# Moving PE drains, moving Gram matmuls, and loading fewer columns in a ConvNeXt V2 block

## The chip, the cores and the metric

The kernel runs on one core of a Trainium2 chip. The metric is the time of one execution on the device in microseconds (us), as the median of several runs. Engines are named as in the profile: PE does matmuls, ACT activations, DVE and POOL elementwise work, SP issues transfers. POOL issues some transfers too, and each issue takes POOL's own time.

Two kinds of numbers appear. Times of kernels are medians of several runs. Places inside a kernel (when a phase starts, how long a block takes) come from the trace of one profiled run, whose span is some 2 us shorter than the time of the same run.

## The reference, cut to what matters

```python
def reference(x, dw, w1, w2, grn_gamma, grn_beta):     # x: 1 x 512 x 512 x 96, bf16
    out = zeros_like(x)
    for i in range(3):
        for j in range(3):
            out = out + xp[:, i:i+H, j:j+W, :] * dw[i, j]   # depthwise 3x3
    h = _layernorm(out, axis=-1)
    h = gelu(einsum('bhwc,ce->bhwe', h, w1))               # 96 -> 384, tanh form
    gx = sqrt((h * h).sum(axis=(1, 2), keepdims=True) + 1e-6)   # over the whole image
    nx = gx / (gx.mean(axis=-1, keepdims=True) + 1e-6)
    h = grn_gamma * (h * nx) + grn_beta + h
    return x + einsum('bhwe,ec->bhwc', h, w2)              # 384 -> 96
```

The sum over the whole image splits the kernel into two phases. Nothing of the last product can be finished before every pixel has been expanded and squared once.

## The kernel before

The image is cut into 128 blocks of four rows. The first phase goes through slots. A full slot convolves one block on PE (`Y`, evacuated by ACT as `y_bf`), and expands an earlier block with `w1` on PE (`U`) and GELU on ACT. The six GELUs of a slot are three `gsh` (channels on partitions, their squares summed by DVE) and three `gm` (pixels on partitions; their squares are summed by Gram matmuls on PE into `SG`). Normalised rows `yn`, and one quarter of the GELU results (`g_dram`), go to DRAM. The last 14 slots have no convolution left.

This is the order of PE's work in a slot (`mlp` part, cut):

```python
conv(0)
if not taps:                      # a slot without convolution
    for b2 in get("gram"):
        if b2 != b:
            gram_mms(b2)          # 12 or 24 matmuls over the gm of the block before
pair(0)                           # U -> gsh0
pair(1)                           # U -> gsh1
squares(0)
conv(1)
...
pair(2)                           # U -> gsh2
...
conv(2)
if evac: evac()                   # y_bf
rest(0)                           # U -> gm0
...
rest(1)
if taps: ... gram_mms(b2) ...     # a slot with convolution has its Gram here
rest(2)
```

`U` has two buffers. Each burst of convolution matmuls uses small tiles (64 rows x 32 columns of PE), the rest uses all 128x128. The burst:

```python
def burst(n):
    k = sum(len(ms) for ms in mms[:n])
    if n:
        pe.drain()
    for h, j, i, dx in mms[n]:
        ...
        pe.matmul(Y[i][32 * j:32 * j + 32, o0:o1], lhsT=Wq[...], rhs=..., ...)
```

The second phase goes through 128 blocks. For each, SP and POOL load what was kept (`gl`), the normalised rows (`ynT`) and the input (`xr`); POOL adds the bias (`xb`); PE expands the three quarters that were not kept (`U`), ACT applies GELU (`gr`), PE multiplies with `W2s` (`O`), DVE adds `xb` (`o_sb`), SP stores. The loads and POOL's addition:

```python
def yn_rows(q):
    return yn_dram[q:q + 2].rearrange("q c w -> (q c) w")[0:128]

def stage_load(n, sq, pq):                      # sq is SP, pq is POOL
    ...
    kept = late.gl.tile([128, 1, NCH, QW], bf16, name="gl")
    (pq if q % 3 == 0 else sq).dma_start(
        out=kept[:].rearrange("p t j w -> p (t j w)"), in_=g_dram[q])
    ynt = yn_ring[v]
    sq.dma_start(out=ynt[:].rearrange("p r w -> p (r w)"), in_=yn_rows(q))
    ...
    xr = late.xr.tile([128, PXP, C], bf16, name="xr")      # 5 buffers
    pq.dma_start(out=xr[:], in_=x[0, r0:r0 + GR]...)
```

A pacing rule decides how far the expansions run ahead of the multiplications. A unit is one third of a block's expansion (one `gr`); there are 384 (`total`), four calls a block, and `LEAD` is 8:

```python
def pace(n, sub):
    due = sum(1 for v in todo if v <= n + 1) if sub == NSUB - 1 else 0
    even = LEAD + (n * NSUB + sub + 1) * total / (NSUB * NBLK)
    advance(max(due, even), n + PRE)
```

## Time and profile before

The time before is 1587.96 us (three runs, 1584.48 to 1589.34).

| Part | From | To | What repeats |
|---|---|---|---|
| Slots with convolution | start | 943 us | 7.54 us a slot |
| 14 slots without | 943 us | 1041 us | mostly 6.80 us a slot |
| Second phase | 1049 us | 1581 us | 4.2 us a block |

The first two lines of the page of before, span and busy time of each engine:

```profile
span 1581.4 us, 55730 instructions
PE 1461.4 (92%) x23749; PEld 845.8 (53%) x23749; DVE 1129.2 (71%) x2027; ACT 1461.4 (92%) x1306; POOL 1316.3 (83%) x933
```

These are averages over parts with different limits. The windows view of before shows two of the parts, one from the slots with convolution and one from the second phase:

```profile
core 0: us, PE busy (x) PEld busy (x) DVE busy (x) ACT busy (x) POOL busy (x), PEclk, DMA share, GB/s
400.00:600.00 200.00, 189.08 (x3402) 95.41 (x3401) 171.96 (x293) 190.46 (x187) 176.73 (x138) 1.00 0.78 240
1100.00:1300.00 200.00, 198.21 (x2780) 143.38 (x2777) 105.92 (x194) 198.32 (x147) 185.10 (x112) 1.00 1.03 411
```

In the second phase, PE and ACT are 99% busy, the DMA engines' share is 1.03 (packets overlap, so it can exceed 1), and POOL is 93% busy.

The timeline view shows order and starts. Its columns are start, duration, engine, line, operation, output and inputs, count, and in brackets the idle time before with its cause. A line may hold several instructions. First PE in a full slot of before:

```profile
600.34 0.87 PE L32 MATMUL Y<-xT,Wq 64*32 64x512 bf16 x24
601.15 1.09 PE L32 MATMUL U<-ynT,w1p 128*128 128x512 bf16 x4
602.35 0.87 PE L32 MATMUL Y<-xT,Wq 64*32 64x512 bf16 x24
```

The first burst ends at 600.34 + 0.87 = 601.21 and the expansion behind it starts at 601.15, 0.06 us earlier. That is a switch of tile size without a drain. The expansion ends at 602.24 and the second burst, which has a drain in front, starts at 602.35, 0.11 us later. Ends of matmuls are not observed: the Trainium skill, "Perfetto Trace Analysis", section "Tensor Engine Instruction (MATMUL, LD_WEIGHTS)", says that the profiler estimates them. So only the difference of the two gaps is used, some 0.17 us. Starts are observed, and over all slots with convolution they say (medians, worked out from the trace): behind a 512-column matmul of an expansion the next matmul starts after 0.22 us where the tile size stays.

ACT in the same slot of before:

```profile
598.75 2.85 ACT L32 ACTIVATE gm<-U 128x1024 bf16<-128x1024 f32 x3
601.84 2.97 ACT L32 ACTIVATE gsh<-U 128x1024 bf16<-128x1024 f32 x3 [0.24 <-ACT gm L32]
604.88 1.45 ACT L32 ACTIVATE y_bf<-Y 128x1536 bf16<-128x1536 f32 x1
```

ACT waits 0.24 us before the first `gsh`, and three `gsh` take 2.97 us where three `gm` take 2.85, so there is a hidden wait among them. One GELU alone has a duration of 1.02 us, but three take 2.85: records of neighbours overlap, and the share of busy time hides short waits.

In the slots without convolution, ACT of before:

```profile
959.03 2.85 ACT L32 ACTIVATE gsh<-U 128x1024 bf16<-128x1024 f32 x3 [3.78 <-issue]
961.76 2.88 ACT L32 ACTIVATE gm<-U 128x1024 bf16<-128x1024 f32 x3
965.83 2.86 ACT L32 ACTIVATE gsh<-U 128x1024 bf16<-128x1024 f32 x3 [1.19 <-issue]
```

ACT waits 1.19 us in front of every `gsh0`. PE's order is the cause. Its timeline in before shows the Gram matmuls (`SG`), which need the last `gm`, in front of the expansion that `gsh0` needs:

```profile
963.77 0.40 PE L32 MATMUL SG<-gm 128*128 128x128 bf16 x4 [0.32 <-ACT gm L32]
964.69 0.62 PE L32 MATMUL SG<-gm 128*128 128x128 bf16 x8 [0.52 <-ACT gm L32]
965.15 1.03 PE L32 MATMUL U<-ynT,w1p 128*128 128x512 bf16 x4
```

In the second phase, POOL of before:

```profile
1179.71 3.14 POOL L277 TENSOR_TENSOR xb<-xr,B2c 128x1536 f32<-128x1536 bf16 x1
1183.14 0.55 POOL L249 DMA_DIRECT2D xr<-in_x_dram  x1 [0.30 <-POOL xb L277]
1183.69 0.54 POOL L244 DMA_DIRECT2D gl<-g_dram  x1
1184.25 3.14 POOL L277 TENSOR_TENSOR xb<-xr,B2c 128x1536 f32<-128x1536 bf16 x1
```

Each issue of `xr` re-uses a buffer that the addition just in front of it has read, so it waits for that addition's semaphore: 0.30 us, on POOL's own work. The Trainium skill, "GPSIMD Engine Reference", section "Instruction dispatch", says that the next POOL instruction may begin before all of the engine's cores are done with the one before, so a dependency needs a wait for the semaphore. The trace agrees: without such a wait, the next instruction starts between 0.07 us before and 0.02 us after the end of the one before; with it, 0.30 us after. The issue itself occupies POOL for 0.55 us.

### The profile page before, as it was taken

To read this page: it belongs to the slowest core of one execution; us is meant where nothing else is said; L and a number is where in the kernel's file an instruction comes from. 1 tells how busy PE (TensorE), PEld (TensorE's weight loads), DVE (VectorE), ACT (ScalarE), POOL (GpSimd) and SP (SyncE) were. 2 spreads that over 40 slices of the span, in tenths; PEclk is the share of its full clock that TensorE was granted. 3 is DMA by queue.
4 is the path that set the end of the run, shared out by engine and by line. 5 is a ranking of instruction groups with operands and counts; after the bars stand their busy time and mean duration, and the time that the engine had idled before them with its cause. 6 is when DMAs were issued, how large, how long until landed. Compare 5 with 4: busy or idle time off the path is not lost. (4 is left out here: it accounts for less than half of the span.)

```text
span 1581.4 us, 55730 instructions
## 1 busy us (share of the span) xinstructions
PE 1461.4 (92%) x23749; PEld 845.8 (53%) x23749; DVE 1129.2 (71%) x2027; ACT 1461.4 (92%) x1306; POOL 1316.3 (83%) x933
## 2 busy tenths in 40 slices
PE   7889999999999999999999986689999999999998
PEld 2434444444444444444444443357777676676766
DVE  6848978888888888888898877755555555555545
ACT  3879999999999999999999997899999999999997
POOL 3559888989989898988989896349999999899997
PEclk8999999999999999999999999999999999999999
DMA  5668787787777787787778666679999999999996
GB/s 146 180 186 264 226 260 212 237 258 227 232 235 246 218 261 222 227 246 239 216 235 254 196 193 200 202 253 412 412 412 412 409 410 408 405 409 408 409 408 259
DMA packets 186654, 444.45 MB, mean 281 GB/s; under 512 B 34054, under 2 KB 83302, under 8 KB 186406
## 3 DMA queue, kind: packets, MB, share of 16 engines
q1 hardware_dynamic: 171156, 373.10, 70.1%
q0 software_dynamic: 13888, 67.64, 10.9%
q8 instruction: 186, 3.05, 0.8%
q14 instruction: 62, 0.51, 0.1%
q10 hardware_dynamic: 1362, 0.15, 0.1%
HBM read 289.30 MB, written 150.72 MB: 278 GB/s over the span
## 5 line engine op out<-in xcount | busy, mean ns | idle before, releaser
L32 PE MATMUL U<-ynT,w1p 128*128 128x512 bf16 x2166 | 606.1, 381 | 17.5 <-ACT gsh L32 13.2
L32 DVE BATCH_NORM_STATS2 bst<-gsh 128x6 f32<-128x512 bf16 x756 | 468.5, 673 | 145.5 <-ACT gsh L32 145.5
L32 ACT ACTIVATE gr<-U 128x1536 bf16<-128x1536 f32 (+1 forms) x384 | 521.1, 1453 | 11.1 <-PE U L32 8.1
L32 POOL TENSOR_TENSOR yn<-y_bf,rbc 128x1536 bf16<-128x1536 bf16 x128 | 397.0, 3104 | 87.0 <-DMA rbc<-r_dram 39.8
L32 DVE TENSOR_TENSOR o_sb<-O,xb 128x384 bf16<-128x384 f32 x512 | 277.4, 556 | 251.2 <-PE O L32 181.2
L277 POOL TENSOR_TENSOR xb<-xr,B2c 128x1536 f32<-128x1536 bf16 x126 | 394.7, 3134 | 47.8 <-DVE B2c L32 44.8
L32 ACT ACTIVATE gsh<-U 128x1024 bf16<-128x1024 f32 x378 | 370.3, 1022 | 50.5 <-ACT gm L32 17.3
L32 ACT ACTIVATE gm<-U 128x1024 bf16<-128x1024 f32 x384 | 367.9, 1032 | 0.1
L32 PE MATMUL Y<-xT,Wq 64*32 64x511 bf16 (+1 forms) x8694 | 323.4, 389 | 35.0 <-DVE B2bc_f L32 3.7
L32 POOL TENSOR_TENSOR ysq<-y_bf 128x1536 bf16<-128x1536 bf16 x114 | 313.1, 2747 | 17.8 <-ACT y_bf L32 17.4
L32 PEld LDWEIGHTS <-w1p 128*128 128x128 bf16 x2166 | 168.1, 98 | 243.7 <-issue 161.0
L32 PEld LDWEIGHTS <-gr 128*128 128x128 bf16 x4584 | 236.3, 98 | 109.1 <-issue 26.4
L32 PE MATMUL O<-W2s,gr 128*128 128x96 bf16 x4584 | 256.8, 206 | 11.0 <-DVE o_sb L32 9.2
L32 PEld LDWEIGHTS <-Wq 64*32 64x32 bf16 x9216 | 105.9, 91 | 227.2 <-issue 188.9
L32 ACT ACTIVATE y_bf<-Y 128x1536 bf16<-128x1536 f32 x121 | 175.5, 1450 | 24.9 <-PE Y L32 17.8
L32 PE MATMUL U<-w1p,ynT 128*128 128x384 bf16 (+2 forms) x1032 | 161.4, 272 | 34.0 <-ACT gm L32 29.9
L32 DVE STREAM_TRANSPOSE xT<-xin 128x576 f32<-128x576 f32 (+1 forms) x256 | 181.4, 747 | 4.0 <-DMA xin<-in_x_dram 3.0
L32 DVE BATCH_NORM_STATS2 bst<-gm 128x6 f32<-128x512 bf16 x252 | 156.5, 676 | 1.5 <-ACT gm L32 1.5
L32 PE MATMUL SG<-gm 128*128 128x128 bf16 x2064 | 139.6, 220 | 11.1 <-ACT gm L32 8.5
L32 PEld LDWEIGHTS <-ynT 128*128 128x128 bf16 x1032 | 88.8, 97 | 90.4 <-issue 69.2
L32 PEld LDWEIGHTS <-gm 128*128 128x128 bf16 x2064 | 120.9, 98 | 23.8 <-ACT gm L32 13.7
L249 POOL DMA_DIRECT2D xr<-in_x_dram x123 | 68.1, 553 | 35.9 <-POOL xb L277 35.6
(103 smaller groups left out, 694.0 us busy)
## 6 DMA issues: line engine op xcount, KB each, us to landing
ynT<-yn_dram SPq DMA_DIRECT2D x126, 512.0 KB
xin<-in_x_dram SPq DMA_DIRECT2D x126, 432.0 KB
yn_dram<-yn SPq DMA_DIRECT2D x512, 96.0 KB
ynT<-yn_dram SPq DMA_DIRECT2D x128, 384.0 KB
xr<-in_x_dram POOLq DMA_DIRECT2D x128, 384.0 KB, 6.7
out_dram<-o_sb SPq DMA_DIRECT2D x128, 384.0 KB
g_dram<-gsh SPq DMA_DIRECT2D x126, 384.0 KB
gl<-g_dram SPq DMA_DIRECT2D x84, 384.0 KB
```

Source lines behind the costliest of these rows:

```text
L32: r = f(*a, **k)
L249: pq.dma_start(out=xr[:], in_=x[0, r0:r0 + GR].rearrange("r w c -> (r w) c").rearrange("(p g) c -> p g c", g=PXP))
L277: pq.tensor_tensor(out=xb[:], in0=grp[q]["xr"][:], in1=bias[:, None, :].to_broadcast([128, PXP, C]), op=ALU.add)
```

## The change

The intent: take the cost of draining PE out of the place where a convolution burst waits to begin; let ACT start the next slot's `gsh0` before Gram is done; load only those columns of `yn` that the second phase expands; spread the expansions so that they last until nearly the end; and store the last block in quarters. Five hunks (cut at each `...`; the new helper `out_part` and the last `stage_out`, which goes, are left out):

```diff
 # columns
     def yn_rows(q):
-        return yn_dram[q:q + 2].rearrange("q c w -> (q c) w")[0:128]
+        k = kept_quads(q) * 128
+        return yn_dram[q:q + 2].rearrange("q c (r w) -> (q c) r w", r=GR)[0:128, :, k:]
 ...
-                sq.dma_start(out=ynt[:].rearrange("p r w -> p (r w)"), in_=yn_rows(q))
+                sq.dma_start(out=ynt[:, :, kept_quads(q) * 128:], in_=yn_rows(q))
 # pacing
-            even = LEAD + (n * NSUB + sub + 1) * total / (NSUB * NBLK)
+            even = LEAD + (n * NSUB + sub + 1) * (total + 2 - LEAD) / (NSUB * NBLK)
 # drains
             def burst(n):
                 k = sum(len(ms) for ms in mms[:n])
-                if n:
-                    pe.drain()
                 for h, j, i, dx in mms[n]:
 ...
                     k += 1
+                if n < 2:
+                    pe.drain()
 # Gram
                 conv(0)
+                pair(0)
+                pair(1)
                 if not taps:
                     for b2 in get("gram"):
                         if b2 != b:
                             gram_mms(b2)
-                pair(0)
-                pair(1)
 # output
+                if n == NBLK - 1:
+                    out_part(q, o_sb, sub)      # stores a quarter of the last block
 ...
+            if n == NBLK - 1:
+                stage_out(*held)                # the block before goes out first
+                held = None
```

More of the change, by code (lines that the diff above doesn't have):

```diff
@@ L885, with out_part @@
         dve2.tensor_copy(out=B2c[:], in_=B2bc_f[:])
+        def out_part(q, o_sb, sub):
+            r0 = q * GR
+            nc.sync.dma_start(
+                out=out[0, r0:r0 + GR].rearrange("r w c -> (r w) c").rearrange(
+                    "(p g) c -> p g c", g=PXP)[:, sub * GPS:(sub + 1) * GPS],
+                in_=o_sb[:, sub * GPS:(sub + 1) * GPS])
         held = None
@@ L896 @@
             held = (q, o_sb)
-        stage_out(*held)
 _INS = ['x', 'dw', 'w1', 'w2', 'grn_gamma', 'grn_beta']
```

## The prediction

It was made without any run of the changed kernel.

> **What bounds the kernel.** Three stages, three limits.
>
> *Phase 1, slots with convolution* (114, until about 940 us). The windows call ACT 95% busy, but its starts in the timeline tell more: back to back, gsh, y_bf and gm start every 0.92, 1.35 and 0.90 us, 6.8 us a slot; the slot takes 7.54. The loop is gm0 -> PE (rest(2), conv 0, pairs 0 and 1, conv 1, pair 2, conv 2) -> y_bf -> gm0: PE's order bounds it, with ACT waits before gsh0 (0.29 us), gsh2 and y_bf.
>
> *14 slots without convolution* (943 to 1041 us): mostly 6.80 us, ACT waiting 1.19 us before each gsh0 (3.78 once): Gram, which needs the last gm, stands before the expansion in PE's order.
>
> *Phase 2* (1049 to 1575 us): DMA shows 1.02, ACT and PE 97 to 99%. But POOL never pauses: xb 3.13 + 0.30 before the xr issue + 0.55 issue, and 0.54 for gl in every third block. The timeline shows 12.54 us per three blocks, 4.18 each, throughout.
>
> **What the change does.**
>
> 1. *Drains.* With a drain, the first conv matmul starts 0.106 us after the modelled end of the expansion before it; at switches without one, either way, the next starts 0.068 us before it. So a drain costs 0.174 us (matmul ends are estimated, says the Trainium skill, "Perfetto Trace Analysis", Tensor Engine Instruction; I use differences). The skill's "TensorEngine Tiling (Array Packing)", Key Properties, says that a change of tiling mode drains anyway; the trace shows the explicit one costs on top. I expect the same price behind a burst: still two per slot. gsh0 starts 0.17 later, gsh2 0.13 later, but y_bf had that slack. Gain: pair 1 now waits about 0.04 us (mean) for its buffer after gm2; this hides inside the moved drain. About 4 us, estimated.
>
> 2. *Gram.* gsh0 follows gm2 at once. With 12 Gram matmuls (9 slots) little wait remains: 5.6 instead of 6.8 us. With 24 (5 slots, 1.5 us) about 0.8 us comes back before gsh2.. Gain about 14 us, all critical.
>
> 3. *Columns.* 512 KB become 384, in 768-byte runs. Packets took 9, 46, 121, 159 ns for 4, 1024, 3072, 4096 bytes: about 37 ns for 768 (estimate), so 1.27 -> 1.17 us of each DMA engine per block, 2% of the DMA load. POOL sets the pace: about 1 us.
>
> 4. *End.* Slower pacing leaves some six more expansions (PE 0.43, ACT 1.35 us each) for the last five blocks, where POOL has no issues left, goes at 3.09 us a block, and PE (4.02) is the limit. The last expansion comes one block before the end: +2.5 and up to +1.8 us. Output in quarters: -1. Net +3 us.
>
> **Sum.** 1588 - 4 - 14 - 1 + 3 = about 1572 us, range 1560 to 1582. Chances: faster by over 2% 0.08, within 2% 0.90, slower 0.02.
>
> **What would show it.** Step 1: waits before gsh0 up by 0.17, before y_bf down, slot 7.50. Step 2: the 1.19 us waits gone, 14 slots in about 84 us. Step 3: DMA share just under 1.0, POOL still 12.54 per three blocks. Step 4: ACT busy until nearly the end.
>
> **What would make it wrong.** Drains that are free behind a burst: up to 0.27 us a slot, 29 us, over 2%. A switch without a drain that costs more after a 512-column expansion: some us lost. 768-byte runs that cost more: phase 2 DMA-bound.

## More of the kernel before

The framework's scheduler may reorder the instructions of one engine in the second phase. In the first phase, the kernel pins them in program order with a wrapper, `InOrder(tc, engine)`.

At the end of before, ACT runs through its last 19 GELUs in 26.4 us, 1.39 us each, without a break:

```profile
1545.35 26.39 ACT L32 ACTIVATE gr<-U 128x1536 bf16<-128x1536 f32 x19 [0.22 <-PE U L32]
```

## The result, and the profile after

The ratio is computed as the mean time of one kernel's fast runs over that of the other's of the same rounds, so it is not quite the ratio of the medians quoted.

| | before | after |
|---|---|---|
| median, four runs each | 1586.40 us | 1567.72 us |
| lowest to highest | 1584.48 to 1589.34 | 1564.99 to 1568.64 |
| ratio (95% interval) | 1 | 0.9878 (0.9856 to 0.9900) |

The change makes the kernel 1.2% faster. The forecast of 1572 us was 4 us too high, inside its range. Where the time went, by the trace (us; `xb` is POOL's addition of one block in the second phase, which comes at a steady rate and so makes a good clock; the first two blocks have theirs some 50 us earlier, and they are not counted):

| | before | after | difference | forecast |
|---|---|---|---|---|
| start to first `xb` | 1049.4 | 1031.1 | -18.3 | -18 |
| the next 100 blocks | 421.7 | 410.5 | -11.2 | about -1 in all |
| from there to the end | 110.2 | 121.6 | +11.3 | +3 |

So the first phase is as forecast, and the second is a near miss for the wrong reasons: two effects, each several times its forecast, cancel.

The page of after:

```profile
span 1563.2 us, 55720 instructions
PE 1450.2 (93%) x23749; PEld 844.8 (54%) x23749; DVE 1129.5 (72%) x2027; ACT 1447.1 (93%) x1306; POOL 1314.2 (84%) x933
```

The work is the same, and only the idle time has shrunk. Windows of after, the same two stretches:

```profile
400.00:600.00 200.00, 188.00 (x3405) 94.88 (x3402) 172.45 (x294) 187.21 (x187) 177.16 (x137) 1.00 0.78 240
1100.00:1300.00 200.00, 200.00 (x2844) 146.90 (x2842) 108.65 (x200) 199.65 (x149) 188.05 (x116) 1.00 1.04 391
```

In the second phase, PE now issues 2844 matmuls where it issued 2780, while the DMA engines move 391 GB/s instead of 411: more blocks, fewer bytes each. The DMA share did not fall below 1 as forecast.

PE in a full slot of after:

```profile
605.72 0.88 PE L32 MATMUL Y<-xT,Wq 64*32 64x512 bf16 x24
606.73 1.03 PE L32 MATMUL U<-ynT,w1p 128*128 128x512 bf16 x4
607.69 0.87 PE L32 MATMUL Y<-xT,Wq 64*32 64x512 bf16 x24
```

The first burst ends at 606.60 and the expansion starts 0.13 us later; the expansion ends at 607.76 and the second burst starts 0.07 us before that. The price has moved from the front of a burst to its back and has kept its size. Over all slots, the first expansion starts 0.501 us after the last matmul of burst 0 has started, 0.32 before; burst 1 starts 0.309 us after the last expansion matmul has started, 0.484 before. So +0.18 and -0.175 (medians of starts, worked out from the trace).

ACT of after, in the same slot:

```profile
604.13 2.85 ACT L32 ACTIVATE gm<-U 128x1024 bf16<-128x1024 f32 x3
607.41 2.92 ACT L32 ACTIVATE gsh<-U 128x1024 bf16<-128x1024 f32 x3 [0.44 <-ACT gm L32]
610.23 1.45 ACT L32 ACTIVATE y_bf<-Y 128x1536 bf16<-128x1536 f32 x1
```

The wait before `gsh0` has grown from 0.24 to 0.44 us, as forecast, and `y_bf` starts 6.10 us after the first `gm`, where it was 6.13. The mean of the regular slots (start of a slot's `gsh` to that of the next, those between 7.2 and 7.9 us, 103 to 107 of 111) went from 7.540 to 7.519 us.

ACT of after, in the slots without convolution:

```profile
955.75 2.95 ACT L32 ACTIVATE gsh<-U 128x1024 bf16<-128x1024 f32 x3
958.60 2.85 ACT L32 ACTIVATE gm<-U 128x1024 bf16<-128x1024 f32 x3
961.31 1.98 ACT L32 ACTIVATE gsh<-U 128x1024 bf16<-128x1024 f32 x2
963.90 1.02 ACT L32 ACTIVATE gsh<-U 128x1024 bf16<-128x1024 f32 x1 [0.62 <-PE U L32]
```

The 1.19 us waits are gone. Behind a slot with 12 Gram matmuls a slot takes 5.55 us; behind one with 24 it takes 6.22, because 0.62 us of the wait returns in front of `gsh2`.

POOL of after, in the second phase:

```profile
1187.61 3.14 POOL L278 TENSOR_TENSOR xb<-xr,B2c 128x1536 f32<-128x1536 bf16 x1
1190.68 0.55 POOL L245 DMA_DIRECT2D gl<-g_dram  x1
1191.23 0.54 POOL L250 DMA_DIRECT2D xr<-in_x_dram  x1
1191.79 3.12 POOL L278 TENSOR_TENSOR xb<-xr,B2c 128x1536 f32<-128x1536 bf16 x1
1195.21 0.55 POOL L250 DMA_DIRECT2D xr<-in_x_dram  x1 [0.30 <-POOL xb L278]
```

This was not forecast and is nowhere in the diff. In before, the issue of `gl` always stood behind that of `xr`. Now, in 28 of 41 places, it stands in front, between the addition and `xr`, and the wait of 0.30 us for the addition disappears behind its 0.55 us. Each such triple of blocks takes 12.18 us (median of the starts of additions three apart) where before it took 12.54 to 12.56.

And the end of after, ACT:

```profile
1528.52 4.13 ACT L32 ACTIVATE gr<-U 128x1536 bf16<-128x1536 f32 x3 [0.51 <-PE U L32]
...
1537.35 4.13 ACT L32 ACTIVATE gr<-U 128x1536 bf16<-128x1536 f32 x3 [1.40 <-PE U L32]
1542.88 4.13 ACT L32 ACTIVATE gr<-U 128x1536 bf16<-128x1536 f32 x3 [1.40 <-PE U L32]
```

ACT waits 1.40 us for PE in every block. PE's timeline in after shows that PE in turn waits for ACT in the same blocks:

```profile
1541.54 0.60 PE L32 MATMUL O<-W2s,gr 128*128 128x96 bf16 x10 [1.13 <-ACT gr L32]
```

The last four blocks take 5.38 to 5.53 us each.

### The profile page after: what moved, and what is told of

The parts are those of the page before. It is cut to its first block, busy times and chain, and to the rows that moved or that the text cites. A ratio compares the mean times of both kernels' runs of the same rounds, so it can differ in the third digit from the quotient of the medians.

```text
span 1563.2 us, 55720 instructions
## 1 busy us (share of the span) xinstructions
PE 1450.2 (93%) x23749; PEld 844.8 (54%) x23749; DVE 1129.5 (72%) x2027; ACT 1447.1 (93%) x1306; POOL 1314.2 (84%) x933
## 5 line engine op out<-in xcount | busy, mean ns | idle before, releaser
L32 PEld LDWEIGHTS <-gr 128*128 128x128 bf16 x4584 | 228.7, 98 | 84.4 <-ACT gr L32 12.1
L32 PE MATMUL O<-W2s,gr 128*128 128x96 bf16 x4584 | 251.3, 206 | 12.1 <-ACT gr L32 9.4
L32 PEld LDWEIGHTS <-Wq 64*32 64x32 bf16 x9216 | 102.2, 90 | 187.5 <-issue 146.9
L32 PE MATMUL SG<-gm 128*128 128x128 bf16 x2064 | 136.3, 219 | 0.5 <-ACT gm L32 0.3
```

The lines of the kernel that those rows point to most:

```text
L32: r = f(*a, **k)
```

## The experiments

Four questions were open. Which hunk makes the second phase's rate? Is that rate POOL's, or do the DMA engines limit it too? What costs 11 us at the end? And are the drains and Gram worth what the sum says? Two theories stood against each other for the rate: that POOL alone sets it (the prediction), and that the DMA engines are a second limit of about the same height.

All kernels gave correct results. All ratios are to before, run in the same job. In the table at the end of this section, the trace of each is cut as above.

### The Gram hunk alone

```diff
                 conv(0)
+                pair(0)
+                pair(1)
                 if not taps: ... gram_mms(b2) ...
-                pair(0)
-                pair(1)
```

> Before plus the Gram move alone. Theory: the 14 slots without convolution lose their 1.19 us wait (0.6 us comes back in the five slots with 24 Gram matmuls), so they take 5.6 to 6.2 us instead of 6.80; first xb of phase 2 starts about 14 us earlier, phase 2 keeps 12.54 us per three blocks, total about -14 us (1572). Rival: part of the 18 us that phase 1 lost came from elsewhere; then this run gains clearly less than 12 us.

Measured: 1569.82 us, ratio 0.9905 (0.9889 to 0.9921). The first `xb` came at 1033.9 us, 15.6 earlier than in before, and the slots took 5.55 and 6.22 us. The next 100 blocks took 423.5 us, no less than in before. The Gram hunk is worth about 15 us, forecast 14, and the second phase does not respond to it. The 14 slots show it with little scatter: from the first of the last 14 `gsh0` to the last, 92.8 to 93.9 us pass in the six kernels with the old order of Gram, and 78.8 to 79.0 us in the eight with the new one.

### The pacing hunk alone

```diff
-            even = LEAD + (n * NSUB + sub + 1) * total / (NSUB * NBLK)
+            even = LEAD + (n * NSUB + sub + 1) * (total + 2 - LEAD) / (NSUB * NBLK)
```

> Before plus the slower pacing alone. Theory: two effects of opposite sign. The scheduler now puts gl before xr on POOL in 28 of 41 places, which takes 28 waits of 0.30 us off POOL (about -10 us in phase 2's pace, 4.18 -> 4.09 us per block), and the lead of the expansions shrinks from 6 to 1 done at the start of a block, so that PE waits for gr in the last 20 blocks (about +13 us). Net within 5 us of before. Rival (intent of the change): pacing spreads work and gains some us, or has no effect; then POOL's period stays 4.18 and no waits of PE for gr appear.

Measured: 1597.07 us, ratio 1.0080 (1.0065 to 1.0095), about 13 us slower: a miss, since within 5 us was expected. This hunk alone moves `gl` in front of `xr` on POOL in 28 places: kernels with the drain, Gram or columns hunk alone have none, nor has the whole change with the old pacing, further down. The diff touches no instruction of POOL, so the order is the scheduler's; why it chooses it was not looked into. But 100 blocks took 416.0 us, 5.7 less than before, not 10. Between 1060 and 1540 us, DVE waited 57 us in all for `o_sb` buffers that a store had not yet released, which in before was rare. From there to the end it took 130.4 us, where before took 110.2. So this hunk carries both the gain and the loss, and the loss outweighs the gain when the full columns are loaded.

### The change with the old pacing

The pacing hunk reversed, all else as in after.

> After with the old pacing. Theory: POOL is back at 12.54 us per three blocks, xb lasts from about 1031 to 1555 us, and the tail from the last xb to the end shrinks from 14.9 to about 6 us: total 1564 to 1567, thus 0 to 4 us faster than after. Rival: the narrower load of yn is what made POOL faster in after; then POOL stays at 4.09 us per block and the total falls by 10 us or more against after.

Measured: 1565.18 us, ratio 0.9885 (0.9868 to 0.9902). The order of POOL went back to that of before. The 100 blocks took 422.1 us and the rest 109.9, against 410.5 and 121.6 in after. So in the full change the pacing hunk gives 11.6 us and takes 11.7. Its balance is nothing.

### POOL's order alone

POOL's loads are pinned in program order, which is `xb`, `gl`, `xr`, with each `xr` now one addition later than the one that frees its buffer. The columns stay full, and the pacing stays old.

```diff
-                (pq if q % 3 == 0 else sq).dma_start(
+                (InOrder(tc, pq) if q % 3 == 0 else sq).dma_start(
 ...
-            pq.dma_start(out=xr[:], in_=...)
+            InOrder(tc, pq).dma_start(out=xr[:], in_=...)
```

> Before with gl pinned in front of xr on POOL and nothing else. Theory: POOL's own order sets phase 2's pace; all 41 waits of 0.30 us in front of xr behind a gl go, POOL's period falls from 4.18 to about 4.06, total about -13 us (1573). Rival: DMA (share 1.02) or ACT sets the pace; then the waits move elsewhere and the total falls by less than 4 us.

Measured: 1585.62 us, ratio 1.0013 (0.9997 to 1.0028). A miss: no gain, where 13 us were expected. (The text expected 41 waits to go; in fact all of them went, as the pinned order leaves a whole addition between an `xr` and the one that frees its buffer. That makes the miss only larger.) The waits view of this kernel between 1060 and 1500 us, with us in total, count and longest:

```profile
DVE o_sb L32 <- DMA out_dram<-o_sb: 52.1, 55, 2.9
POOL xb L277 <- DVE o_sb L32: 39.0, 74, 2.4
```

POOL, freed of its own waits, now waits for DVE; DVE waits for stores to leave its four output buffers. The same view of before shows POOL as the one waited for, and only 5.6 us on stores:

```profile
DVE o_sb L32 <- POOL xb L277: 47.3, 44, 1.7
POOL xr L249 <- POOL xb L277: 31.2, 105, 0.3
DVE o_sb L32 <- DMA out_dram<-o_sb: 5.6, 4, 1.9
```

The rate barely moved, from 421.7 to 417.5 us for 100 blocks, and the rest took 6.5 us longer. There is a second limit at nearly the same height, and it shows as stores that come late. The theory that POOL alone sets the rate falls.

Why the stores come late is to be seen in the queue of SP, which issues both these stores and the loads of `yn`. The waits view of order alone for SP, same window:

```profile
SPq L247 <- DMA ynT<-yn_dram: 113.3, 90, 3.4
SPq L307 <- DMA out_dram<-o_sb: 72.0, 72, 2.6
```

SP waits for earlier transfers to land before it issues the next, 226 us of these 440 in all, and so it issues a store up to 2.9 us after the block's last `o_sb`. The other traces fall into two groups. In all six kernels with full columns SP waits 171 to 244 us for transfers (195 in before), in all eight with the narrower load 0 to 5 us, and there no store is issued more than 0.5 us after its `o_sb`. So with full columns the transfers were late already in before, although DVE hardly waited for a store there.

### The columns hunk alone

```diff
-                sq.dma_start(out=ynt[:].rearrange("p r w -> p (r w)"), in_=yn_rows(q))
+                sq.dma_start(out=ynt[:, :, kept_quads(q) * 128:], in_=yn_rows(q))
```
(with the narrower `yn_rows`)

> Before plus the narrower load alone. After the order run, the theory is: phase 2 has two limits of almost the same height, POOL's own 4.18 us per block and DMA at about 4.17 us per block with full columns; lifting one alone gains nothing. Then this run stays at 12.54 us per three blocks with POOL never idle, DMA load per block falls, total -2 to 0 us (1582 to 1584). Rival: DMA was the limit and POOL only followed; then the block falls to 4.1 us or less and the total by 8 us or more.

Measured: 1585.24 us, ratio 0.9994 (0.9975 to 1.0013); 421.7 us for 100 blocks, exactly as before. Fewer bytes alone bring nothing: POOL still sets the rate. What they do change is SP's waits for transfers, from 195 us to none.

### Columns and order together

Both edits above, nothing else.

> Before plus the narrower load plus gl pinned in front of xr. Theory of two limits: each alone gave nothing, together the block falls from 4.18 to about 4.06 us, and the total by 10 to 15 us (1570 to 1574). Rival: a third limit (PE and ACT at 4.03 to 4.15) already holds, or the DMA load of 768-byte runs is no lower; then the total stays within 4 us of before.

Measured: 1566.24 us, ratio 0.9876 (0.9856 to 0.9896), some 20 us less than before, more than the 10 to 15 expected, by two edits which bring nothing alone. 100 blocks took 403.6 us. The windows view of this kernel:

```profile
1100.00:1300.00 200.00, 200.00 (x2833) 147.14 (x2831) 111.01 (x199) 200.00 (x150) 188.27 (x117) 1.00 1.04 392
```

ACT and PE never pause, and a block takes 4.03 us, three times ACT's interval of 1.343 us between two `gr`. No single interval between 1100 and 1480 us is longer than 1.355 us, so ACT runs at its own pace and is now the limit. PE is hardly lower: by the shortest spacings of its matmuls, a block is some 3.96 us of PE (estimate from this trace). The four kernels make a clean square (us for 100 blocks):

| | POOL order as before | POOL order pinned |
|---|---|---|
| all columns (512 KB) | 421.7 | 417.5 |
| needed columns (384 KB) | 421.7 | 403.6 |

The DMA share was 1.03 or 1.04 in all four, so the share does not tell which of them the DMA engines hold back. The time of the packets per block does not either: it was 4.28 us of each DMA engine in before and 4.29 in columns alone, at the same pace; with fewer bytes, packets of 3072 bytes took 128 ns instead of 124 (means over the 100 blocks). SP's waits do tell. The narrower load consists of four times as many packets as the full one, so it is not the number of packets that held SP up.

### The drains hunk alone

```diff
-                if n:
-                    pe.drain()
                 for h, j, i, dx in mms[n]: ...
+                if n < 2:
+                    pe.drain()
```

> Before plus the moved drains alone. Theory: a drain costs 0.174 us on either side, gsh0 starts about 0.18 us later, y_bf and the slot come 0.02 to 0.05 us earlier in 114 slots: -2 to -5 us, phase 2 unchanged. Rival: the drain behind a burst is free, or the gain of phase 1 in after is only Gram's; then -15 us or more, or 0.

Measured: 1581.93 us, ratio 0.9970 (0.9953 to 0.9988): 0.3%, 4.8 us by the means, with an interval of about 2 to 7 us. The profiled run reached its first `xb` only 0.7 us earlier, and the 100 blocks took 421.7 us, as in before. The slots fix the size better than the times: the mean of the regular slots is 7.539 to 7.541 us in the six kernels with the drains in front, and 7.514 to 7.519 us in the eight with the drains behind. That is 0.02 us a slot, some 2.4 us in all, at the low end of what was expected.

### The change with all columns

The columns hunk reversed, all else as in after.

> After with the full load of yn. Theory of two limits: the order that the pacing brings frees POOL, but DMA holds the block at 4.18 to 4.20 us until the starved tail: total about 1577 to 1580, thus 9 to 13 us slower than after. Rival: the load's width does nothing, as I predicted (about 1 us).

Measured: 1578.73 us, ratio 0.9942 (0.9919 to 0.9965). After had 0.9878, so the columns are worth about 10 us in the full change, not 1. (The two ratios are of two jobs, and two of the six runs here took 1573 us, the others 1578 to 1581; so the 10 is rough.) The waits view of this kernel between 1060 and 1500 us:

```profile
DVE o_sb L32 <- DMA out_dram<-o_sb: 55.4, 41, 3.0
```

In after this wait is absent from the same view. Where POOL's order is freer, the stores are what full columns delay.

### The change with old pacing and POOL pinned

This is after with the pacing of before and with the pinned loads of the order experiment. It follows from all of the above: keep what gives, drop what takes.

> After with the old pacing and with the POOL issues of phase 2 pinned in program order (no wait in front of xr). Theory: the parts add now: Gram -14, drains -5, columns with POOL freed -19, output in quarters -1: 1545 to 1550, phase 2 at 4.03 us per block, which is ACT's 3 x 1.343. Rival: phase 2's gain from a freed POOL needs phase 1 as it was, or the parts overlap; then over 1555.

Measured: 1549.50 us, ratio 0.9772 (0.9748 to 0.9796), faster than before by 2.3% and about 1.1% better than after (0.9772 against 0.9878, which is from another job). POOL of this kernel, which now has slack in front of its additions:

```profile
1181.85 0.55 POOL L32 DMA_DIRECT2D xr<-in_x_dram  x1
1182.68 3.12 POOL L278 TENSOR_TENSOR xb<-xr,B2c 128x1536 f32<-128x1536 bf16 x1 [0.28 <-DVE o_sb L32]
```

And ACT at its end, 30 GELUs without a break:

```profile
1498.88 40.42 ACT L32 ACTIVATE gr<-U 128x1536 bf16<-128x1536 f32 x30
```

### The same with the new pacing

Only the pacing formula differs from the kernel before this one.

> After with only the POOL issues pinned, so that it differs from the run before in the pacing formula alone. Theory: the lead of the expansions shrinks to nothing, PE waits for gr in the last 20 blocks: 5 to 10 us slower than the run with the old pacing. Rival: with a freed POOL the spread pacing works as intended; then faster than the run with the old pacing.

Measured: 1560.71 us, ratio 0.9846 (0.9822 to 0.9869), 11.2 us slower by the medians, somewhat more than expected. ACT at its end:

```profile
1540.33 4.13 ACT L32 ACTIVATE gr<-U 128x1536 bf16<-128x1536 f32 x3 [1.40 <-PE U L32]
```

The rest after the first 100 blocks took 127.4 us against 111.5; the 100 blocks before took 400.7 against 403.6. The new pacing borrows 3 us early and pays 16 back late. What happens is a shrinking lead. The old formula lets 8 units of lead stand from start to end. The new one spreads 378 units over the same 512 calls, so that the lead falls from 8 units to 2. In the trace of after, 6 units stand ready ahead of PE when it begins block 5, 3 at block 80, and 1 or 2 from block 108 on. The time between the last `gr` of a block and PE's first use of it falls with it: 6.4 us at block 5, 2.8 at block 60, 0.8 at block 96, and at block 104 it is negative. From there on PE stands still until ACT has delivered, and because PE runs in order, it meanwhile does not issue the expansions that ACT needs next. Both wait in turn, and a block takes 4.2, then 4.5, 4.6 and at last 5.5 us instead of 4.03.

### A milder pacing

```diff
-            even = LEAD + (n * NSUB + sub + 1) * (total + 2 - LEAD) / (NSUB * NBLK)
+            even = LEAD + (n * NSUB + sub + 1) * (total + 4 - LEAD) / (NSUB * NBLK)
```

> As the run before, with total + 4 - LEAD in place of total + 2 - LEAD, so that four expansions of lead remain at the end where two did. Theory: the starvation begins under about three expansions of lead, so here it hardly appears, and the last ACT work ends about 1.3 blocks nearer to the end: 0 to 4 us faster than the old pacing. Rival: any shrinking lead costs; then slower than the old pacing.

Measured: 1548.87 us, ratio 0.9776 (0.9750 to 0.9801), the same as with the old pacing (against before, this is unclear at the 2% mark: the interval crosses it). Two units more of lead at the end are enough: the time between the last `gr` and its use never fell below 0.17 us, and no block took over 4.07 us among the last ten. So the loss is not a matter of how evenly work is spread, but of whether the lead reaches zero. And in these two runs there was nothing to win by spreading either.

### The last block stored as a whole

The best kernel, without the output hunk.

> The run with the old pacing and pinned issues, without the output in quarters. Theory: the end is 1 to 1.5 us later, since the last write carries 384 KB where 96 KB did. Rival: no difference beyond noise (0.5 us).

Measured: 1552.07 us, ratio 0.9789 (0.9766 to 0.9812). From the last `o_sb` to the end, 3.42 us passed, against 2.57 with quarters: 0.85 us, where 1 to 1.5 was expected. (All traces agree: 3.42 to 3.53 us as a whole, 2.55 to 2.57 in quarters.) The medians differ by 2.6 us, but the intervals overlap, and the two profiled runs differ by 1.2 us already at the first `xb`. The trace settles the 0.85; the times cannot.

### All traces side by side

| Kernel | first `xb` | next 100 blocks | rest | span |
|---|---|---|---|---|
| before | 1049.4 | 421.7 | 110.2 | 1581.4 |
| after | 1031.1 | 410.5 | 121.6 | 1563.2 |
| Gram alone | 1033.9 | 423.5 | 109.9 | 1567.3 |
| pacing alone | 1049.1 | 416.0 | 130.4 | 1595.4 |
| after, old pacing | 1030.3 | 422.1 | 109.9 | 1562.3 |
| order alone | 1049.2 | 417.5 | 116.7 | 1583.3 |
| columns alone | 1051.1 | 421.7 | 109.9 | 1582.6 |
| columns and order | 1047.9 | 403.6 | 112.3 | 1563.8 |
| drains alone | 1048.8 | 421.7 | 110.5 | 1580.9 |
| after, all columns | 1033.6 | 415.5 | 128.7 | 1577.8 |
| after, old pacing, pinned | 1033.0 | 403.6 | 111.5 | 1548.1 |
| after, pinned | 1032.6 | 400.7 | 127.4 | 1560.7 |
| after, mild pacing, pinned | 1031.1 | 402.3 | 112.8 | 1546.2 |
| after, old pacing, pinned, whole output | 1034.2 | 405.2 | 112.3 | 1551.7 |

Kernels with the same first phase differ by up to 4 us at the first `xb` (after and the six variants with all of its first phase: 1030.3 to 1034.2). That is the scatter that a single trace carries; one slot near the start, at 70 us, took 36 to 40 us in the 14 traces. By the means of these seven and of the five kernels with the first phase of before (1049.3), the first phase gained 17 us rather than the 18.3 of the single pair.

## Why the prediction was right or wrong

1. **Drains: right in mechanism; the gain was rather 2 us than 4.** "I expect the same price behind a burst", 0.174 us: measured 0.175 to 0.18 on either side. "About 4 us": by the times between 2 and 7, by the slots some 2.4. The Trainium skill, "TensorEngine Tiling (Array Packing)", section "Key Properties", says that a change of tiling mode drains PE anyway. The trace shows that the explicit drain costs on top of that, and keeps its price wherever it stands. The gain comes from the slack of the place it was moved to. The regular slot came out at 7.52 us, not at the 7.50 that was given.

2. **Gram: right.** "Gain about 14 us, all critical": about 15 alone. "About 0.8 us comes back" in the long slots: 0.62. Drains and Gram together were to give 18, and the first `xb` came 18.3 us earlier in the pair of traces, 17 by the means of all.

3. **Columns: the step that failed is "POOL sets the pace: about 1 us".** For the hunk alone it held, with a measured effect of nothing. But it took POOL's order as given. The pacing hunk changed POOL's order through the scheduler, and with that POOL was no longer the only limit: with all columns the DMA engines hold the second phase at nearly the same height (417.5 us for 100 blocks with POOL freed, against 421.7), and with fewer columns they do not (403.6). The trace of before had it: SP waited 195 of 440 us for transfers to land. The prediction looked at POOL and at the DMA share only. In the full change the columns are worth about 10 us. The prediction's tests in the profile also failed: triples of blocks on POOL went from 12.54 to 12.18 us where the order had changed, and the DMA share stayed at 1.04 instead of falling "just under 1.0", and at 1.03 even where fewer bytes came at an unchanged pace (columns alone). The cost of a packet was right: 36 to 37 ns for 768 bytes in the trace, 37 estimated.

4. **End: right in sign, but the term "net +3 us" was mis-sized.** The terms +2.5 and +1.8 counted the expansions that would be left for the last blocks. They left out that PE runs in order, so when the lead runs out, PE and ACT wait for each other in turn, and not in the last five blocks but in the last twenty. The loss measured 11.7 us (after against after with old pacing) and 11.2 (with POOL pinned). The quarters were right: 0.85 us, estimated 1.

5. **The sum was right by cancellation.** -4 -14 -1 +3 gave 1572 us. The trace says -18.3 -11.2 +11.3. A forecast that lands within 0.3% says little about its parts if two of its errors have the same size and opposite signs.

What stays open: with full columns SP waits for transfers, stores are issued late, and a quarter fewer `yn` bytes cures both; whether the bytes of the loads themselves or the queue that loads and stores share on SP sets this limit was not separated (no run issues the stores from another engine). Traces of before and of the kernels with Gram, drains or columns alone, or old pacing, have one stall of 2.5 us at the same place in the second phase, with POOL waiting for PE; it was not explained. It makes up 2.5 of the 421.7 us, so the steady rate there is 4.19 us a block. How the scheduler arrives at POOL's order was not looked into; the runs show only which hunk triggers it.

## What to carry to other kernels

When a stage has an engine that never pauses, look for the second limit before pricing a change: relieve both alone and together, because two edits which bring nothing alone may bring 20 us as a pair. Where the DMA share stands at 1 whatever one does, look at what the issuing queue waits for. Compare the order of instructions on each engine before and after a change, also on engines that the diff does not touch, and pin an order that matters. A lead between two engines must not reach zero before the end; spreading work "evenly" gains nothing while the slower engine is already full, and costs as soon as an in-order engine has to stop for it.

## What the Trainium skill lacked or had wrong

- "TensorEngine Tiling (Array Packing)", "Key Properties", states that a mode switch drains PE, but has no price, neither for the switch nor for an explicit drain at it. Here, by starts, the switch cost some 0.09 us (0.309 us against 0.22), and an explicit drain 0.175 to 0.18 us on top, the same in front of a burst and behind it.
- "GPSIMD Engine Reference", "Instruction dispatch", says that a dependent POOL instruction needs a wait for a semaphore, but not what it costs: here 0.30 us after the end of the instruction waited for, where an independent one started 0.07 us before that end. It occurred 120 times in before.
- "Perfetto Trace Analysis", "DMA Optimizations", warns of an overhead of transfers under 2 KB; the section itself has no number for it. In the second phase, a packet of 768 bytes took 36 ns (median; mean 37), and one of 3072 bytes 121 (mean 124), so some 19% more for each byte. To load a quarter fewer bytes in such runs still took SP's waits for transfers from 195 us to none (before against columns alone).
